# Attention over memory slots and a gated feed-forward: the sum of batch 3's nine exponentials on GpSimd, and two denominator products in place of nine

## The chip, the cores and the metric

The kernel runs on one core of a Trainium2 chip. The metric is the device time of one execution in microseconds (us). The core's engines are called PE (TensorE, matrix products), PEld (its weight loads, which run beside the products), DVE (VectorE), ACT (ScalarE), POOL (GpSimd) and SP (SyncE, which issues transfers). On-chip memory is SBUF; PE writes its results into PSUM, which has eight banks.

## The reference

There are 8 batches, 8 heads, 576 positions of 64 elements, and 32 memory slots. Per batch and head:

```python
a = exp(phi - max(phi)); a = a / (sum(a over slots) + 1e-09)
k_m = einsum('bhsm,bhsd->bhmd', a, k)        # keys of the 32 memory slots
v_m = einsum('bhsm,bhsd->bhmd', a, v)        # values of the 32 memory slots
attn = softmax(q @ k_m.T / 8)
x = attn @ v_m                               # heads side by side: 4608 x 512
out = (silu(x @ w_gate) * (x @ w_val)) @ w_out   # 512 -> 1536 -> 512
```

The kernel has its own placement of these sums: it lays heads out as 64 rows of nine positions each, and forms for every head pair and memory slot the sum of the exponentials over positions, which it calls the denominators. They scale the memory keys and values once, when these leave PSUM.

## The kernel before

**Layout.** `phi` of a batch is a tile of 128 partitions with four head pairs and nine positions (JK = 9). `phi_exp` (L170, ACT at L172) makes the exponentials `t_ephi`, 128 x (9 x 4 x 32), in bf16. A product of PE with `ones2` (two columns, one for each half of the partitions) sums them over the partitions: `kv_denominators` (L239, product at L258) does so for each of the nine positions and accumulates in PSUM, nine products of a 128 x 128 weight and two columns. `kv_sum` (L222, L230) forms the memory keys and values, 72 small products in two banks `p_kv`. `kv_reciprocal` (L260, DVE at L262) inverts the denominators and `kv_norm` (L268, DVE at L266) scales keys and values with them on their way to SBUF as `t_bkv`; `kv_T` (L278) transposes them.

**The short form.** `phi_sum(b)` (L205) lets POOL add the nine exponentials ahead of PE. Four adds at L212 (4 against 4 positions, then 2 against 2, 1 against 1, and the ninth) give one 128 x 128 sum `t_es` in fp32; a cast (L218) writes its high part and a subtract (L219) its low part, both bf16, into `t_ehl`. `kv_denominators` then makes two products, of the high and of the low part. A copy of one element, a mark (`wait_for`, L645), stands ahead of the adds, so that POOL begins with them only when the second normalised attention `t_A` of the batch in work (L452 on DVE) is there. Before the change batches 4, 6 and 7 have this form; 2, 3 and 5 make nine products; 0 and 1 have a form of their own.

**Order.** The order of each engine's instructions is written out by hand. From batch 2 on, a loop (L996) handles batch b: scores and their exponentials, sums and normalisation of the attention (L452), then the gates. `gv_gate` (L524) makes the gate and value products (L515), ACT the silu (L532), DVE the product `t_h` (L538). 24 such slots are spread with other streams by `spread` (L852): the output products of the batch before (L727), and at slots 6 to 10 `kv_items(b + 1)`, the denominators, key sums and transposes of the next batch. `kv_items` (L292) takes them in one of three ways. With a `beside` and no sum from POOL (`own`), the denominators come first, in a bank of their own `p_S`, followed by the key sums; the projections that `beside` carries (`u_item`, L472, whose results ACT and DVE copy at L492 and L496) come after. With a sum from POOL (`behind`) the key sums come first, then `beside`, then the two products into a free corner of a key bank.

**Queues.** A finished chunk of the hidden layer calls `chunk_done` (L586), which puts sums `t_S` on POOL (L603, L560), whose results the output products read, and, at chunk 1 of batch b, the loads of batch b + 3 on POOL's queue (L982: q, phi, k, v). In batch 2 POOL ends with the loads of batch 4 (L1020) ahead of the gates.

**Banks.** PSUM banks are handed out in turn from a list (L75); who takes a bank waits until its last reader is done.

Of the kernel before, what the change touches and what calls it, by code (L numbers as in the profile page):

```python
# [14 lines left out]
def kernel(  # L15
# [59 lines left out]
    def bank(shape, dtype, name):  # L75
        tag = free.pop(0)
        t = ps.tile(shape, dtype, tag=tag, name=name)
        held[id(t)] = tag, t
        return t

    def done(*tiles):

        for t in tiles:
            free.append(held.pop(id(t))[0])
# [29 lines left out]
    def load_qT(b):  # L114

        qTs[b] = att.tile([128, NS, 128], BF16, tag="qT", name="t_qT")
        nc.sync.dma_start_transpose(out=qTs[b], in_=qs[b])
# [52 lines left out]
    def phi_exp(b):  # L170
        t = att.tile([128, JK, NP, M], BF16, tag="ephi", name="t_ephi")
        nc.scalar.activation(  # L172
            out=t.rearrange("p j i m -> p i j m"),
            in_=phis.pop(b).rearrange("p i (j m) -> p i j m", m=M),
            func=AF.Exp,
        )
        ephis[b] = t
# [25 lines left out]
    esums = {}  # L203
# [18 lines left out]
    def kv_sum(b, p, parts):  # L222


        w0, w1 = parts[0], parts[-1] + 1
        n = (w1 - w0) * D
        for j in range(JK):
            for i in range(NP):
                for g in range(NG):
                    nc.tensor.matmul(  # L230
                        p[g][32 * i:32 * i + 32, 0:n],
                        lhsT=phi_of(b, g, j, i),
                        rhs=kvs[b][64 * g:64 * g + 64, w0:w1, i, j * D:(j + 1) * D],
                        start=(j == 0),
                        stop=(j == JK - 1),
                        tile_position=(64 * g, 32 * i),
                    )

    def kv_denominators(b, p):  # L239

        if b in masked:
            for g in range(NG):
                for j in range(JK):
                    nc.tensor.matmul(
                        p[:, g:g + 1],
                        lhsT=masked[b][:, j, g].rearrange("p i m -> p (i m)"),
                        rhs=ones1,
                        start=(j == 0),
                        stop=(j == JK - 1),
                    )  # L250
            return
        if b in esums:
            hl = esums.pop(b)
            terms = [hl[:, t] for t in range(2)]
        else:
            terms = [ephis[b][:, j].rearrange("p i m -> p (i m)") for j in range(JK)]
        for n, x in enumerate(terms):
            nc.tensor.matmul(p, lhsT=x, rhs=ones2, start=(n == 0), stop=(n == len(terms) - 1))  # L258

    def kv_reciprocal(b, p):  # L260
        r = att.tile([128, NG], FP32, tag="rS", name="t_rS")
        nc.vector.reciprocal(out=r, in_=p)  # L262
        rSs[b] = r
# [4 lines left out]
    def kv_norm(b, p):  # L268

        t = att.tile([128, 3, 128], BF16, tag="bkv", name="t_bkv")  # L270
        for g in range(NG):
            x = p[g][:, 0:D].rearrange("p (a d) -> p a d", a=1).to_broadcast([128, 2, D])
            scaled_copy(t[:, g].rearrange("p (a d) -> p a d", a=2), x, rSs[b][:, g:g + 1])
            scaled_copy(t[:, 2, D * g:D * g + D], p[g][:, D:2 * D], rSs[b][:, g:g + 1])
            done(p[g])
        bkvs[b] = t

    def kv_T(b):  # L278


        kTs[b] = att.tile([128, 3, 128], BF16, tag="kT", name="t_kT")
        t = bkvs.pop(b)
        if b > 3:
            nc.sync.dma_start_transpose(out=kTs[b], in_=t.rearrange("p n x -> p (n x)"))
            return
        p = bank([128, 3, 128], BF16, "p_T")
        for n in (2, 0, 1):
            nc.tensor.transpose(p[:, n], t[:, n], ident)
        nc.vector.tensor_copy(out=kTs[b], in_=p)
        done(p)  # L290

    def kv_items(b, beside=None):  # L292


        def run_sums():
            o = 2 * D
            behind = b in esums
            own = beside and not behind
            if own:
                d = bank([128, NG], FP32, "p_S")  # L300
                kv_denominators(b, d)
                kv_reciprocal(b, d)
                done(d)
            p = [bank([128, CH], FP32, f"p_kv{g}") for g in range(NG)]
            if not (own or behind):
                kv_denominators(b, p[0][:, o:o + NG])
            kv_sum(b, p, (0, 1))
            if behind:
                beside()
                kv_denominators(b, p[0][:, o:o + NG])  # L310
            if not own:
                kv_reciprocal(b, p[0][:, o:o + NG])
            kv_norm(b, p)
            if beside and not behind:
                beside()

        return [run_sums, lambda: kv_T(b)]
# [511 lines left out]
    def q_items(b, evac):  # L829
        return [lambda n=n: q_T(b, n, evac[n]) for n in range(3)]  # L830
# [30 lines left out]
    def exp_tables():  # L861
        nc.scalar.preload_act_table_set("natural_log_exp_and_others")
# [133 lines left out]
    for b in range(2, B):  # L996
        last = b + 1 == B
        exp_tables()
        if b == 2:
            load_qT(3)  # L1000
            phi_exp(2)
            (zero, ops0), (one, ops1) = products(0, ("c11",)), products(1, ("p1", "c11"))
            kv, q2 = kv_items(2), q_items(2, "aaa")
            run(zero[:6])
            sums = {n: f for n, f in zip(((1, 1), (0, 2), (1, 2)), late)}
            late.clear()
            sums[0, 2]()
            weight_sums(0)
            weight_sums(1)
            run(zero[6:12] + one[:6] + kv[:1] + q2[:2])  # L1010
            weight_sums(2, (0, 1))
            run(zero[12:16] + zero[18:22] + kv[1:] + q2[2:] + zero[16:18] + zero[22:24])
            weight_sums(2, (2, 3))
            ops0["c11"]()
            ops1["p1"]()
            wait_for(Ts[2][0:1, 3, 0, 0:1])
            for part in ((0, 1), (3,), (2,)):
                for c in (1, 2):
                    sums[1, c](part)
            loads(4)  # L1020
            backlog = one[6:12] + zero[36:] + one[12:36]
            ops = ops1
        else:
            run(take(6))
        for g in range(NG):
            scores(b, g)
        if b > 2:
            ops["p1"]()
            u_values(b)
        else:  # L1030
            run(zero[24:36] + take(6))
        run(take(6))
        z_inv_v(b, 0)
        ops["c11"]()
        run(take(6))
        if not last:
            phi_exp(b + 1)
        z_inv_v(b, 1)
        if b > 2:
            norm(b, 0)  # L1040
            norm(b, 1)
        run(take(6))
        run_late()
        if b == 4:
            wait_for(atts[4, 1][0:1, 0, 0:1])
            quad_sums(0)
        nc.scalar.preload_act_table_set("silu_and_others")
        run(take(6))
        if b == 2:
            norm(2, 0)  # L1050
        run(take(6))
        if b == 2:
            norm(2, 1)
            u_three(2)
            run(one[36:])
        g = gv_slots(b)
        quad = []
        if b == 4:
            quad = products(b, (), 0)[0]
        if last:  # L1060
            rest, rest_ops = products(b, (), 1)
            backlog += rest[:12]
        beside = 0 if last else 2 if quad else min(4, len(backlog))
        outs = [lambda: run(take(1)) for _ in range(len(backlog) - beside)]
        streams = [(g, 0, 24), (quad[:12], 0, 3), (quad[12:], 12, 18.5)]
        streams += [(outs, 4, 7 if quad else 24)]
        if b == 2:
            streams += [([lambda: u_values(2)], 2.5, 3)]
        if last:
            streams += [([u_item(b, 2)], 5, 6)]  # L1070
        if not last:
            if b > 2:
                load_qT(b + 1)
            if b > 2 and b != 4:
                phi_sum(b + 1)
            streams += [
                (kv_items(b + 1, lambda: (u_item(b, 2, "aava")(), run(take(2)))), KV, KV + 4),
                ([lambda: (u_three(b + 1), run(take(2)))], 19, 20),
            ]
        spread(*streams)  # L1080
        flush_mul()
        units, ops = products(b, ("p1", "c11"))
        backlog += units
# [34 lines left out]
```

## Time and profile before

| what | value |
|---|---|
| three timed runs | 233.22, 233.81, 233.97 us; median 233.81 |
| span of the profiled execution, first to last instruction | 231.4 us |
| its own time | not given apart; the three runs are 1.8 to 2.5 us above the span |
| mean granted TensorE clock | 0.997 |
| denominator products of batch 3 | 79.98 us from the start of the span |
| POOL idle between batch 4's loads and the first sum of batch 2 | 8.75 us, up to 83.84 us |

Times within the span count from its first instruction. A row of the timeline merges equal instructions that follow each other, and gives the start, the time from the first start to the last end, the engine, the line, the operation with what it writes and reads, and the count; in brackets stands the idle time of the engine ahead of the row, and whose end ended it. Matmuls are pipelined, so that their durations overlap: how long a product holds PE is read from the distance of the starts, not from its duration.

### The profile page before, as it was taken

What the parts mean: (1) busy time and instruction counts of PE and PEld (TensorE: products, weight loads), DVE (VectorE), ACT (ScalarE), POOL (GpSimd) and SP (SyncE); (2) the same over time, 40 slices, a digit from 0 to 9 for tenths busy, and PEclk for the clock granted to TensorE, in tenths of its full rate; (3) what the DMA queues carried; (4) which work ended last, traced back from release to release, by engine and by line L of the source; (5) the groups of instructions that cost most, each with busy time, mean ns of one, the idle gap of its engine ahead of it and who ended that gap; (6) DMA issues with size and microseconds to landing.
All of it is one profiled execution on the core that took longest, in us unless ns stands there. A gap on an engine that the chain in (4) does not pass through costs nothing.

```text
span 231.4 us, 7210 instructions
## 1 busy us (share of the span) xinstructions
PE 221.6 (96%) x2825; PEld 169.8 (73%) x2825; DVE 185.1 (80%) x423; ACT 171.7 (74%) x365; POOL 140.8 (61%) x190
## 2 busy tenths in 40 slices
PE   6987799999999999999999999999999999999993
PEld 2544476778887777878788787887788778878882
DVE  4245789999966799989997668998999899977732
ACT  2777898988447989968896658978898789677310
POOL 8422427998199049765977689464845394039291
PEclk9999999999999999999999999999999999999998
DMA  6999999999996992999299946994014502202125
GB/s 214 210 211 206 199 207 207 221 245 268 205 225 175 256 256 49 223 204 184 71 223 191 226 134 115 252 236 89 28 65 114 104 0 95 91 10 84 31 85 160
DMA packets 36674, 36.84 MB, mean 159 GB/s; under 512 B 14624, under 2 KB 31008, under 8 KB 36640
## 3 DMA queue, kind: packets, MB, share of 16 engines
q0 software_dynamic: 16272, 22.42, 52.5%
q1 hardware_dynamic: 19600, 13.18, 22.9%
q10 hardware_dynamic: 768, 0.79, 1.1%
q8 instruction: 22, 0.36, 0.6%
q14 instruction: 12, 0.10, 0.1%
HBM read 42.47 MB, written 9.44 MB: 224 GB/s over the span
## 4 chain that ended last, share of the span: by engine, by line
PE 86%; DMA 9%; POOL 2%; ACT 1%; issue 0%; DVE 0%; POOLq 0%
PE p_g L515 21%; PE p_os L727 21%; PE p_v L515 20%; PE p_oc L727 10%; DMA W<-in_moe_w_val_dram 9%; PE p_oa L727 5%; PE p_u L472 5%; PE p_kv L230 2%; PE p_g L396 1%; POOL t_kv L99 1%; POOL t_kv L103 1%; PE p_q L383 0%; POOL t_q L108 0%; ACT t_qT L337 0%; POOL W L138 0%
## 5 line engine op out<-in xcount | busy, mean ns | idle before, releaser
L538 DVE TENSOR_TENSOR t_h<-t_sg,p_v 128x288 bf16<-128x288 bf16 x192 | 81.8, 451 | 14.1 <-PE p_v L515 7.0
L515 PEld LDWEIGHTS <-t_U 128*128 128x128 bf16 x768 | 73.9, 98 | 21.2 <-issue 3.5
L532 ACT ACTIVATE t_sg<-p_g 128x288 bf16<-128x288 f32 x192 | 73.3, 424 | 17.1 <-PE p_g L515 11.4
L515 PE MATMUL p_g<-t_A,t_U 128*128 128x288 bf16 x384 | 77.0, 286 | 0.0
L515 PE MATMUL p_v<-t_A,t_U 128*128 128x288 bf16 x384 | 77.0, 286 | 0.0
L727 PEld LDWEIGHTS <-t_S 128*128 128x128 bf16 x384 | 37.5, 98 | 4.5 <-issue 0.2
L603 POOL TENSOR_TENSOR t_S<-t_h 128x512 bf16<-128x512 bf16 x17 | 19.7, 1157 | 32.7 <-DVE t_h L538 31.2
L727 PEld LDWEIGHTS <-t_h 128*128 128x128 bf16 x288 | 27.1, 98 | 8.6 <-issue 5.0
L492 ACT CAST t_U<-p_u 128x512 bf16<-128x512 f32 x51 | 27.0, 605 | 6.6 <-PE p_u L472 6.6
L727 PE MATMUL p_os<-t_T,t_S 128*128 128x256 bf16 x192 | 23.7, 273 | 0.0
L560 POOL TENSOR_TENSOR t_S<-t_S,t_h 128x512 bf16<-128x512 bf16 x17 | 19.6, 1156 | 1.3
L560 POOL TENSOR_TENSOR t_S<-t_h 128x512 bf16<-128x512 bf16 x16 | 18.4, 1152 | 0.0
L560 POOL TENSOR_TENSOR t_S<-t_h,t_S 128x512 bf16<-128x512 bf16 x16 | 18.4, 1152 | 0.0
L472 PE MATMUL p_u<-W,t_kT 64*32 64x512 bf16 (+1 forms) x416 | 15.3, 363 | 1.2 <-DMA W<-in_moe_w_gate_dram 0.6
L496 DVE CAST t_U<-p_u 128x512 bf16<-128x512 f32 x21 | 13.6, 683 | 1.9 <-PE p_u L472 1.9
L727 PE MATMUL p_os<-t_T,t_h 128*128 128x256 bf16 x96 | 14.8, 273 | 0.0
L875 PE MATMUL p_warm<-bones 128*128 128x512 bf16 x44 | 12.5, 421 | 1.7 <-DVE bones L897 1.7
L452 DVE TENSOR_TENSOR t_A<-t_E,t_lz 128x576 bf16<-128x576 bf16 x16 | 11.4, 740 | 0.7 <-ACT t_lz L428 0.7
L727 PE MATMUL p_oc<-t_T,t_S 128*128 128x256 bf16 x96 | 11.9, 273 | 0.0
L727 PE MATMUL p_oa<-WO,t_h 128*128 128x256 bf16 x96 | 11.8, 273 | 0.0
L727 PE MATMUL p_oc<-WO,t_S 128*128 128x256 bf16 x96 | 11.8, 272 | 0.1
L727 PE MATMUL p_os<-WO,t_h 128*128 128x256 bf16 x96 | 11.8, 273 | 0.0
(107 smaller groups left out, 308.3 us busy)
## 6 DMA issues: line engine op xcount, KB each, us to landing
out_dram<-t_o SPq DMA_DIRECT2D x11, 512.0 KB, 3.0
t_kv<-in_k_dram POOLq DMA_DIRECT2D x8, 576.0 KB, 10.5
t_q<-in_q_dram POOLq DMA_DIRECT2D x8, 576.0 KB, 8.4
t_kv<-in_v_dram POOLq DMA_DIRECT2D x8, 576.0 KB, 14.7
t_phi<-in_phi_dram POOLq DMA_DIRECT2D x6, 576.0 KB, 8.1
out_dram<-t_o SPq DMA_DIRECT2D x10, 256.0 KB, 4.5
WO<-in_moe_w_out_dram POOLq DMA_DIRECT2D x3, 512.0 KB, 19.2
W<-in_moe_w_gate_dram POOLq DMA_DIRECT2D x2, 512.0 KB, 16.5
```

Of the source, the lines that this page charges most:

```text
L230: nc.tensor.matmul(p[g][32 * i:32 * i + 32, 0:n], lhsT=phi_of(b, g, j, i), rhs=kvs[b][64 * g:64 * g + 64, w0:w1, i, j * D:(j + 1) * D], st ...
L452: nc.vector.tensor_tensor(out=a, in0=es.pop((b, g)), in1=lzs.pop((b, g)), op=ALU.mult)
L472: nc.tensor.matmul(p[g][32 * i:32 * i + 32, o:o + n], lhsT=kTs[b][64 * g:64 * g + 64, 2, 32 * i:32 * i + 32], rhs=w_part(w, c, i, g, halve ...
L492: nc.scalar.copy(out=t, in_=p)
L496: nc.vector.tensor_copy(out=t, in_=p)
L515: nc.tensor.matmul(p[:, 0:HALF], lhsT=Us[b, c, g][:, o // 2, which, 128 * (o % 2):128 * (o % 2 + 1)], rhs=atts[b, g][:, r], start=(g == 0) ...
L532: nc.scalar.activation(out=sg, in_=gate[:, 0:HALF], func=AF.Silu)
L538: nc.vector.tensor_tensor(out=dst, in0=sg, in1=val[:, 0:HALF], op=ALU.mult)
L560: eng.tensor_tensor(out=out, in0=x, in1=y, op=ALU.subtract)
L603: eng.tensor_tensor(out=t[:, 0], in0=A21, in1=A22, op=ALU.add)
L727: nc.tensor.matmul(mine[home][:, u], lhsT=lhs(c, m, u), rhs=rhs(c, m), start=fresh and u == 0, stop=(k == 5), skip_group_check=u == 1 or n ...
L875: nc.tensor.matmul(p[:, 0:128 * a], lhsT=bones, rhs=x.to_broadcast([128, a, 128]) if a > 1 else bones, start=True, stop=True,)
```

## The change

Two conditions change.

```diff
         def run_sums():
             o = 2 * D
-            behind = b in esums
+            behind = b in esums and b != 3
             own = beside and not behind
...
         if not last:
             if b > 2:
                 load_qT(b + 1)
-            if b > 2 and b != 4:
+            if b != 4:
                 phi_sum(b + 1)
```

The second lets `phi_sum(3)` run in batch 2, ahead of the 24 slots. The first keeps batch 3 in the `own` order although it has a sum from POOL: the denominators ahead of the key sums, in bank `p_S`. Since `esums` now holds batch 3, `kv_denominators(3)` makes two products from `t_ehl` in place of nine from `t_ephi`. All other batches keep their form.

## The prediction

> **What bounds the kernel now.** I read the busy shares of the page first, then the chain that ended last, then the timelines of TensorE (PE), GpSimd (POOL) and VectorE (DVE) around the change, and last the groups of the tiles concerned.
>
> The page of the kernel before, its busy shares and its chain of work by engine:
>
> ```profile
> PE 221.6 (96%) x2825; PEld 169.8 (73%) x2825; DVE 185.1 (80%) x423; ACT 171.7 (74%) x365; POOL 140.8 (61%) x190
> ...
> PE 86%; DMA 9%; POOL 2%; ACT 1%; issue 0%; DVE 0%; POOLq 0%
> ```
>
> PE is busy for 96% of the span and is 86% of the chain; the DMA share is the first weights, before 26.75 us. In the 40 slices the granted PE clock is 9 in all but the last. From 27 us to the last products near 227 us the group view shows idle time before PE groups of 0.6 us in all, 0.5 of it at the first projections. So a matmul that is taken away in between moves the end by its own place in the stream, and a wait put there moves it by its length. POOL at 61% is off the chain.
>
> PE at the place of the change, timeline of the kernel before (start us, duration us, engine, line, operation, count; one row merges equal instructions that follow each other):
>
> ```profile
> 79.73 0.41 PE L515 MATMUL p_v<-t_A,t_U 128*128 128x288 bf16 x2
> 79.98 0.37 PE L258 MATMUL p_S<-ones,t_ephi 128*128 128x2 bf16 x9
> 80.28 0.80 PE L230 MATMUL p_kv<-t_kv,t_ephi 64*32 64x128 bf16 x72
> 80.86 0.66 PE L472 MATMUL p_u<-W,t_kT 64*32 64x512 bf16 x16
> ```
>
> The nine denominator products stand in a bank of their own already, ahead of the 72 key sums, with no idle time before them. The order of PE's instructions in the two built kernels differs by 14 rows, seven weight loads and seven matmuls, all here; the order of banks is the same.
>
> **PE's part.** The nine last 0.37 us together and one alone 163 ns (the group of L258), so eight steps take 0.207 us: 26 ns from one to the next; the single starts, 79.978, 80.007, 80.032 up to 80.182, give 25. From the ninth start to the first key sum (80.275) are 93 ns, a change of tile shape that stays. So 9 to 2 products saves 7 x 25 ns = **0.175 us**, if nothing makes PE wait. The second product would then start at 80.007 and the key sums at 80.10.
>
> A row sets the far end. A weight load of L258 lasts 95 to 98 ns. If the loads could not overlap, seven would be worth 7 x 96 ns = 0.67 us. The starts 25 ns apart speak against it, so I take 0.175 and keep 0.67 for the low end of the range.
>
> [...]
>
> **Does the earlier end reach the end of the kernel?** After the key sums the next waits are for banks. Ends of DVE and ACT (ScalarE) work against PE starts, singly in the trace: the projections (L472) at 80.86 to 81.09 take banks that were free by 80.01, 80.13, 80.38 and 80.44, at least 0.65 us before each start; the bank of the second key sum was freed 0.45 us before it. A shift of 0.175 fits into these. The tightest comes later: the weight load at 82.17 comes 0.05 us after the last normalisation (L266) ended at 82.11. That chain shifts too, because its first instruction waits for the key sums themselves:
>
> ```profile
> 80.66 0.16 DVE L262 RECIPROCAL t_rS<-p_S 128x2 f32<-128x2 f32 x1
> 81.12 0.99 DVE L266 TENSOR_SCALAR t_bkv<-p_kv,t_rS 128x128 bf16<-128x128 f32 x4 [0.30 <-PE p_kv L230]
> ```
>
> DVE stands idle for 0.30 us here until the key sums end, and the reciprocal is over at 80.82. With key sums 0.175 earlier it starts at 80.95, still after the reciprocal. ACT's next copies (81.39, idle 0.95 us before) wait for PE as well. So the whole wave moves, and behind it every stage is paced by PE.
>
> **POOL's part.** The order view puts seven instructions on POOL: a mark (L645), four adds (L212), a cast (L218) and a subtract (L219), between the batch-4 loads and the first sum t_S of batch 2 (L603). The first two rows below are these neighbours; the others are the same seven instructions where batch 4 has them now:
>
> ```profile
> 74.34 0.76 POOL L103 DMA_DIRECT2D t_kv<-in_v_dram  x1
> 83.84 1.15 POOL L603 TENSOR_TENSOR t_S<-t_h 128x512 bf16<-128x512 bf16 x1 [8.75 <-DVE t_h L538]
> ...
> 99.54 0.18 POOL L645 COPY t_mark<-t_A 1x1 bf16<-1x1 bf16 x1 [2.49 <-DVE t_A L452]
> 99.68 1.15 POOL L212 TENSOR_TENSOR t_es<-t_ephi 128x512 f32<-128x512 bf16 x1
> 100.91 1.26 POOL L212 TENSOR_TENSOR t_es<-t_es 128x256 f32<-128x256 f32 x2
> 102.25 0.43 POOL L212 TENSOR_TENSOR t_es<-t_es,t_ephi 128x128 f32<-128x128 f32 x1
> 102.74 0.29 POOL L218 CAST t_ehl<-t_es 128x128 bf16<-128x128 f32 x1
> 103.11 0.43 POOL L219 TENSOR_TENSOR t_ehl<-t_es,t_ehl 128x128 bf16<-128x128 f32 x1
> ```
>
> From the mark's start to the end of the cast are 103.03 - 99.54 = 3.49 us, to the end of the subtract 103.54 - 99.54 = **4.00 us** (3.99 and 4.00 in batches 6 and 7). POOL has an idle gap of 8.75 us to hold it. The mark waits for the second normalisation of batch 2:
>
> ```profile
> 74.90 0.75 DVE L452 TENSOR_TENSOR t_A<-t_E,t_lz 128x576 bf16<-128x576 bf16 x1
> ```
>
> It ends at 75.65. In batch 4 that instruction ended at 99.41 and the mark began at 99.54, 0.13 later; 0.13 in batches 6 and 7 too. So the mark starts at 75.78, the high part (cast) is there at 79.27 and the low part (subtract) at **79.78**. The exponentials themselves (L172) were done at 72.04.
>
> PE loads the high part at 79.86 (the first L258 load of before) and the low part at 79.98 (the second). The margins are 0.59 and **0.20 us**. A releaser's end to PE's start takes between 0.05 us (the product at 75.04 after DVE's 74.99) and 0.13 (DVE to POOL above), so 0.07 to 0.15 us remain. It is narrow, but I cost the wait at nothing. If that cover is gone, PE stands for what is missing, with all 72 key sums behind the waiting load in its queue.
>
> How sure is 4.00? POOL's 66 sums of t_S last 1142 to 1172 ns under whatever DVE and ACT do beside them, so 2% or 0.08 us is the spread to expect. That leaves the margin at about zero in the worst case, hence a lost gain of up to 0.1 us. What this stage has and batch 4 has not is two DVE casts (L496, 75.57 to 76.85) beside the first adds. If each blocked POOL for its whole 0.68 us, the low part would come at 81.14. The nearest rows say no: POOL sums beside the three casts at 88.64 to 90.52 last 1.15 to 1.16. I take nothing, and keep 1.36 us as the upper end.
>
> [...]
>
> Queued behind the mark on POOL is the L603 sum at 83.84. POOL would be free at 79.78, 4.06 us ahead of it; without that cover its sums and the batch-5 loads at 91.47 would be late by what is missing. No DMA is added or moved; SP's order is the same. DVE beside such adds is not slowed: six products of L538 take 2.91 us from 100.64, 455 ns each, as they do at 79.56 with POOL idle. The buffer of these exponentials is written again by batch 5 at 120.2, long after POOL's last read.
>
> **Sum.** 0 on POOL, DVE, ACT and SP, -0.175 on PE: the span goes from 231.4 to 231.3 us. Three times are given, 233.22 to 233.97, none named as that of the profiled execution; what lies around the span is 1.8 to 2.5 us, 2.4 by the median, and doesn't change. So **233.6 us** against 233.81.
>
> **Rivals.**
> 1. *The products' loads are worth their full length.* 0.67 us less, 233.1. For it: the 96 ns of a load. Against: the 25 ns between starts, and PEld is at 73%, not the limit.
> 2. *The low part arrives a little late or PE's queue runs dry at the wait.* With 0.1 to 0.4 us of standing the gain is used up: 233.7 to 234.0. For it: a margin of 0.07 to 0.15 us, and PE now has to take up 144 loads and matmuls of key sums straight behind a wait. Against: three chains of 3.99 to 4.00.
> 3. *Slower: the two casts block POOL.* Place: the first adds, 75.8 to 78. Low part at 81.14, PE starts its load 0.05 later, 81.14 + 0.05 - 79.98 = 1.21 us of standing, less 0.175: +1.03, 234.8. It decides once the chain is longer than 4.00 + 0.15 + 0.175, some 4.3 us, and passes 0.3% (0.70 us) at some 5.0. Against: the sums beside casts above.
> 4. *The change doesn't do what it says*, nine products kept: excluded by the order of instructions.
>
> **Chances.** Forecast 0.78, rival 1 0.05, rival 2 0.10, rival 3 0.07. A change of 0.3% is about what a measurement of this kernel can tell from no change: 233.11 and 234.51 are its bounds. Forecast and rival 2 lie within; rival 1 is on the lower bound and counts as faster, rival 3 as slower: 0.05, 0.88, 0.07. The range: the runs of before lie 0.59 below to 0.16 above their median, which makes 233.0 to 233.8 of the forecast; rival 2 and the same scatter extend it to 234.2, rival 1 lies inside, rival 3 outside.
>
> **What would show it.** Right: a mark near 75.8 and L219 ending near 79.8 on POOL; two L258 products from 79.98 with no idle time before the weight loads; key sums at 80.10; the projections at 88.09 0.17 earlier, and so to the end. Wrong: a PEld wait on POOL at L258, an L212 of over 1.2 us, L538 above 460 ns beside it, or a later PE wait that takes the 0.17 back.

## The result, and the profile after

The changed kernel takes 232.91 us (median of 17 runs, 232.83 to 233.39); the kernel before, run beside it, 233.41 (17 runs, 233.14 to 233.97). The ratio is **0.9982** (95% interval 0.9976 to 0.9988): 0.42 us less, between 0.28 and 0.56 (the medians lie 0.50 apart). The forecast was 0.175 us less. The size is wrong by a factor of 2.4, and the 233.6 us also stood on a median of three runs, 233.81, that 17 runs put at 233.41.

The page after, the busy shares and the chain by engine:

```profile
PE 222.2 (96%) x2818; PEld 169.8 (73%) x2818; DVE 184.9 (80%) x423; ACT 171.7 (74%) x365; POOL 144.3 (62%) x197
...
PE 86%; DMA 9%; POOL 2%; ACT 1%; issue 0%; DVE 0%; POOLq 0%
```

PE has seven products less and POOL seven instructions more, 3.5 us of work; the shares are as before. PE at the place of the change, timeline after:

```profile
79.67 0.41 PE L515 MATMUL p_v<-t_A,t_U 128*128 128x288 bf16 x2
79.91 0.19 PE L258 MATMUL p_S<-ones,t_ehl 128*128 128x2 bf16 x2
80.03 0.80 PE L230 MATMUL p_kv<-t_kv,t_ephi 64*32 64x128 bf16 x72
80.62 0.66 PE L472 MATMUL p_u<-W,t_kT 64*32 64x512 bf16 x16
```

Two products, no idle time ahead of them, and the key sums 0.12 us after the first (0.30 before). This execution reaches the stretch 0.064 us earlier than that of before, an amount that it has from the very start, ahead of 26 us. From the first gates to the key sums it needs 0.177 us less, and from there to the last product 147.05 us as before. DVE behind it:

```profile
74.84 0.75 DVE L452 TENSOR_TENSOR t_A<-t_E,t_lz 128x576 bf16<-128x576 bf16 x1
80.59 0.16 DVE L262 RECIPROCAL t_rS<-p_S 128x2 f32<-128x2 f32 x1
80.88 0.99 DVE L266 TENSOR_SCALAR t_bkv<-p_kv,t_rS 128x128 bf16<-128x128 f32 x4
```

The idle time ahead of the normalisation, 0.30 us, is gone: it starts 0.24 us earlier, with the key sums. The normalised attention `t_A`, for which POOL's mark waits, ends at 75.59. POOL after:

```profile
74.27 0.76 POOL L103 DMA_DIRECT2D t_kv<-in_v_dram  x1
75.65 0.18 POOL L645 COPY t_mark<-t_A 1x1 bf16<-1x1 bf16 x1 [0.62 <-DVE t_A L452]
75.79 1.15 POOL L212 TENSOR_TENSOR t_es<-t_ephi 128x512 f32<-128x512 bf16 x1
77.02 1.25 POOL L212 TENSOR_TENSOR t_es<-t_es 128x256 f32<-128x256 f32 x2
78.35 0.43 POOL L212 TENSOR_TENSOR t_es<-t_es,t_ephi 128x128 f32<-128x128 f32 x1
78.85 0.29 POOL L218 CAST t_ehl<-t_es 128x128 bf16<-128x128 f32 x1
79.21 0.43 POOL L219 TENSOR_TENSOR t_ehl<-t_es,t_ehl 128x128 bf16<-128x128 f32 x1
83.59 1.15 POOL L603 TENSOR_TENSOR t_S<-t_h 128x512 bf16<-128x512 bf16 x1 [3.95 <-DVE t_h L538]
```

The chain takes 79.64 - 75.65 = 3.99 us beside the two casts. It ends at 79.64, 0.27 us ahead of the load that needs it (79.91), and POOL still waits 3.95 us for its next sum.

So the two profiles show the forecast 0.18 us at its place and nothing more between 27 and 227 us. The other 0.24 us of the ratio are not in these two executions.

### The profile page after: what moved, and what is told of

It is laid out like the page before. It is cut to its first block, busy times and chain, and to the rows that moved or that the text cites. A ratio compares the mean times of both kernels' runs of the same rounds, so it can differ in the third digit from the quotient of the medians.

```text
span 231.1 us, 7204 instructions
## 1 busy us (share of the span) xinstructions
PE 222.2 (96%) x2818; PEld 169.8 (73%) x2818; DVE 184.9 (80%) x423; ACT 171.7 (74%) x365; POOL 144.3 (62%) x197
## 4 chain that ended last, share of the span: by engine, by line
PE 86%; DMA 9%; POOL 2%; ACT 1%; issue 0%; DVE 0%; POOLq 0%
PE p_g L515 21%; PE p_os L727 21%; PE p_v L515 20%; PE p_oc L727 10%; DMA W<-in_moe_w_val_dram 9%; PE p_oa L727 5%; PE p_u L472 5%; PE p_kv L230 2%; PE p_g L396 1%; POOL t_kv L99 1%; POOL t_kv L103 1%; PE p_q L383 0%; POOL t_q L108 0%; ACT t_qT L337 0%; POOL W L138 0%
## 5 line engine op out<-in xcount | busy, mean ns | idle before, releaser
L515 PEld LDWEIGHTS <-t_U 128*128 128x128 bf16 x768 | 73.9, 98 | 21.2 <-issue 3.5
L515 PE MATMUL p_g<-t_A,t_U 128*128 128x288 bf16 x384 | 77.0, 286 | 0.0
L515 PE MATMUL p_v<-t_A,t_U 128*128 128x288 bf16 x384 | 77.0, 286 | 0.0
L875 PE MATMUL p_warm<-bones 128*128 128x512 bf16 x44 | 13.5, 447 | 1.7 <-DVE bones L897 1.7
```

Of the source, the lines that this page charges most:

```text
L515: nc.tensor.matmul(p[:, 0:HALF], lhsT=Us[b, c, g][:, o // 2, which, 128 * (o % 2):128 * (o % 2 + 1)], rhs=atts[b, g][:, r], start=(g == 0) ...
L875: nc.tensor.matmul(p[:, 0:128 * a], lhsT=bones, rhs=x.to_broadcast([128, a, 128]) if a > 1 else bones, start=True, stop=True,)
```

## The experiments

**Theories.** Theory 1: PE's 0.18 us is all, and the rest is scatter. Theory 2: something else of the change gives 0.2 to 0.3 us, by POOL's work (2b) or by the missing PE instructions (2a). Theory F, formed after the first two sets: PE's instructions come to it by transfers, and in part of the runs of the kernel before one of these comes late; the change moves the place where it is needed. Each set of runs has its own runs of the kernel before on the same chip, and each ratio is to these; not every set has runs of the changed kernel.

### Controls and halves

Before again: no edit.

> The kernel before, unchanged, against itself: how far two sets of runs of one kernel lie apart on this chip. All theories: ratio 1.000, with the interval across 1. If it lies beside 1 by 0.05% or more, a difference of the size of 0.1 us cannot be put down to a change at all.

Measured: 1.0004 (0.9991 to 1.0018). The changed kernel again:

> The changed kernel once more. In its first profile the PE stream is 0.18 us shorter at the denominators of batch 3, as predicted, while the time fell by 0.42 us (ratio 0.9982, 0.9976 to 0.9988). Theory 1 (the change is worth the 0.18 us of PE alone, and the rest is scatter of the parts ahead of 26 us and behind 227 us, which differs from one set of runs to the next): ratio near 0.9992, anywhere from 0.998 to 1.000. Theory 2 (something of the change outside the PE stretch gives 0.2 to 0.3 us more, each time): 0.9982 again, and the profile again shows it in the same part.

Measured: 0.9982 (0.9973 to 0.9991), 233.12 us. So the size repeats. PE's part without POOL's (seven of batch 3's nine positions are left out of the sums):

```diff
-            terms = [... for j in range(JK)]
+            terms = [... for j in range(2 if b == 3 else JK)]
```

> The kernel before, with the denominators of batch 3 summed from two positions of nine: seven of nine are left out, and POOL adds nothing. Theory 1: as the changed kernel, 0.18 us less on PE, ratio near 0.9992. Theory 2a (the extra comes from seven fewer PE instruction pairs): as the changed kernel, 0.9982. Theory 2b (the extra comes from POOL's work): 0.9992 while the changed kernel stays at 0.9982.

Measured: 0.9981 (0.9971 to 0.9991). POOL's part without PE's:

```diff
+            if b != 4:
                 phi_sum(b + 1)
+            if b == 2:
+                esums.pop(3)
```

> The kernel before, with POOL's sum of the exponentials of batch 3 made in batch 2 as in the change, but not used: batch 3 keeps its nine products. Theory 1 and 2a: ratio 1.000, PE's stream unchanged to 0.02 us. Theory 2b: 0.9988 to 0.9990, that is 0.25 us less without any product saved. Rival 3 of the prediction (POOL and DVE in each other's way): slower, L538 or L496 longer by more than 10 ns beside the adds.

Measured: 1.0003 (0.9988 to 1.0017). POOL's work alone gives nothing that these runs can tell, and costs nothing; the whole 0.42 to 0.44 us come with the seven missing PE products. Theory 2b falls, 2a stands.

The profile of this run with POOL's sum alone fell on a run of 234.40 us, and shows where such runs lose their time. PE there, and in the kernel before at the same place:

```profile
134.92 0.41 PE L515 MATMUL p_v<-t_A,t_U 128*128 128x288 bf16 x2
136.29 0.71 PE L727 MATMUL p_oc<-t_T,t_Q 128*128 128x256 bf16 x5 [0.97 <-issue]
```

```profile
134.85 0.41 PE L515 MATMUL p_v<-t_A,t_U 128*128 128x288 bf16 x2
135.09 0.71 PE L727 MATMUL p_oc<-t_T,t_Q 128*128 128x256 bf16 x5
```

From one row's start to the next are 1.37 us in place of 0.24: PE stands for 1.13 us, and the bracket names no engine and no transfer of data, but issue, the profile's word for a wait whose cause it doesn't show. Theory F holds that PE lacks its own instructions. The page lists a queue for instructions:

```profile
q8 instruction: 22, 0.36, 0.6%
```

These are 22 transfers of 16,384 bytes; PE's list has 5668 rows in the trace, so one for about every 258; two places at which PE stands, both shown below, lie 768 numbers and three transfers apart, which makes 256. That they carry PE's instructions is inferred from these numbers and from what follows. Their times are in the trace. The one that starts at 132.3 in the kernel before lands at 133.51, and the instruction at 135.09, number 3522 in PE's list, runs without delay; in the run of 234.40 us it starts at 133.73, lands at 134.97, and number 3522 runs at 136.29. In the changed kernel the list is 14 shorter ahead of this point, so that number 3522 is seven products later in the work, at 135.64:

```profile
135.40 0.41 PE L515 MATMUL p_g<-t_A,t_U 128*128 128x288 bf16 x2
135.64 0.41 PE L515 MATMUL p_v<-t_A,t_U 128*128 128x288 bf16 x2
```

Landing of that transfer and first use of number 3522, us, in nine of the profiles:

| profile | number 3522 as in | landing | use | between | PE stands there |
|---|---|---|---|---|---|
| before | before | 133.51 | 135.09 | 1.59 | 0 |
| before again | before | 133.66 | 135.16 | 1.51 | 0 |
| POOL's sum alone | before | 134.97 | 136.29 | 1.32 | 1.13 |
| two products, seven more early | before | 133.96 | 135.28 | 1.32 | 0.28 |
| nine, seven more early | work 14 places later | 133.95 | 135.25 | 1.30 | 0.78 |
| the same again | work 14 places later | 131.79 | 134.42 | 2.63 | 0 |
| after | after | 133.41 | 135.64 | 2.23 | 0 |
| after again | after | 133.67 | 135.76 | 2.09 | 0 |
| after, third | after | 134.34 | 135.89 | 1.55 | 0 |

In the three profiles in which PE stands here, it stands at number 3522, which is another product where the list ahead of it is longer, and goes on 1.30 to 1.32 us after the landing; no profile shows a shorter distance at this number. The kernel before has 0.2 to 0.3 us to spare over that, the changed one 0.2 to 0.9. In all other profiles of this case, those of the sections below included, the distance is 1.73 us or more. In all, three of the seven profiles with the list of before or a longer one show PE standing there, and none of the eleven with a shorter list. The run of 234.40 us less its 1.13 us is 233.27, as the profiled run of before again (233.28), in which PE doesn't stand.

The place matters because PE uses up its list unevenly. From number 3266, 256 places ahead, PE takes 6.04 us to number 3522 in the kernel before and 6.72 in the changed one: with seven products fewer ahead, the first of these places comes 0.11 us later in the work, since small products stand there (72 key sums in 0.73 us), and the second 0.79 us, since large ones do (two of L515 in 0.24 us).

### Moving the list of instructions

If F holds, it is the place in the list that counts, not the product saved. The warming products are products of PE on a constant, which `warm` issues while inputs are on their way; `warm(104)` makes 26 of them, 512 columns wide, and a second argument asks for that many of 128 columns. Seven warming products less at the start, nine denominator products kept:

```diff
-    warm(104)
+    warm(76)
```

> The kernel before with its nine products, and seven of the 26 warming products at the start of PE (ahead of 9 us, while the inputs are on their way) taken away, so that everything behind them stands 14 places earlier in PE's list of instructions, as it does in the changed kernel. Theory F (fetch): PE's instructions come in 22 transfers of 16 KB, and in the kernel before the instruction at 135.1 us is the first of such a transfer, which landed 1.5 to 1.6 us ahead of it, and in one profile 1.3 us ahead with PE standing for 1.13 us; with 14 places less that first instruction comes 0.5 to 0.6 us later in the work, and the standing goes. It expects 0.2 to 0.3 us less than before (ratio 0.9987 to 0.9992) although no product of batch 3 is saved, no run above 233.7, and 2.0 us or more between landing and use. Theory 1 (PE's 0.18 us and scatter): ratio 1.000. If the shorter warming lowers the granted clock, it is slower by a us or more and the run tells nothing.

Measured: 1.0014 (0.9999 to 1.0028), an expectation missed. In its profile the first gates start at 27.80 us, 0.6 late, behind weights that came late (PE waits 1.25 us for them, 0.52 in the kernel before); from the key sums of batch 3 on it takes 147.06 us, with 2.56 from landing to use. The start spoilt it, and the time says nothing of F. Seven more in the changed kernel:

```diff
-    warm(104)
+    warm(111, 7)
```

> The changed kernel with seven narrow products more among the warming ones at the start, so that the work behind batch 3 stands at the same places in PE's list of instructions as in the kernel before. Theory F: the 0.18 us of the seven products stay, the rest goes: ratio to before 0.9992 (233.3 where before has 233.5), scattered runs above 233.8 return, 1.5 to 1.6 us between landing and use at 135. Theory 2a without the fetch (fewer products give 0.43 us in some other way): 0.9982 as the changed kernel.

Measured: 0.9992 (0.9983 to 1.0002), 233.25 us, with one run at 233.92. Its profile shows PE standing again:

```profile
134.76 0.41 PE L515 MATMUL p_v<-t_A,t_U 128*128 128x288 bf16 x2
135.28 0.71 PE L727 MATMUL p_oc<-t_T,t_Q 128*128 128x256 bf16 x5
```

0.52 between the rows in place of 0.24. F gave 0.9992, the products alone in another way 0.9982, which the interval leaves out by little; it does not leave out 1.000, and this set has no runs of the changed kernel. The same edit in the kernel before:

> The kernel before with seven narrow products more at the start: 14 places later in PE's list. Theory F: the first instruction of that transfer is now needed some 0.7 us earlier, near 134.4, 0.8 to 0.9 us after the landing where 1.3 are needed, so PE stands in every run, 0.4 us at the least, and more where the transfer is late: ratio 1.002 to 1.004, and the profile shows idle PE ended by issue near 134.4. Theory 1 and any theory without the fetch: ratio 1.000.

Measured: 0.9995 (0.9986 to 1.0003), against F. Its profile was of its longest run, 234.23 us, and there number 3522, seven products earlier in the work and due at 134.4, does wait, for 0.78 us:

```profile
134.25 0.38 PE L727 MATMUL p_os<-t_T,t_Q 128*128 128x256 bf16 x2
135.25 0.38 PE L727 MATMUL p_os<-t_T,t_Q 128*128 128x256 bf16 x2 [0.62 <-issue]
```

The other eleven, 233.07 to 233.66, leave no room for such a wait: the lowest run of the kernel before in this set is 233.09. (The 0.86 us of the next expectation is the whole stretch behind the key sums; 0.08 of it arises near 111.5 us, in the repeat as well.) Once more, for a profile of one of those:

> The kernel with seven narrow products more at the start once more. Its first 12 runs contradicted theory F: median 0.1 us below before in place of 0.4 to 0.9 above, although its one profile (a run of 234.23) shows PE standing for 0.86 us at 134.4, 1.30 us after the landing. Theory F, kept: a profile of a run near 233.3 shows the transfer landing at 133.0 or earlier, so that 1.3 us remain. Theory F, fallen: a run near 233.3 with the landing at 133.5 as in the kernel before and no standing.

Measured: 0.9995 (0.9984 to 1.0006). The profiled run, 233.36 us, had the landing at 131.79, as F needs. In this run the transfer started at 130.86, some 1.5 us ahead of its start in the kernel before; I had held that start for fixed, and the size that F gave for these two sets is refuted with it: the place alone doesn't say how long PE stands. The attempt to shorten the list at the other end of the start:

```diff
     z_inv(1, 0)
-    warm(8)
     z_inv(1, 1)
     norm(1, 0)
-    warm(16)
+    warm(4)
     v_direct(1, "vvvv")
-    warm(8)
```

> The kernel before with nine products and seven of the 512-wide warming products between 21 and 25 us left out (the first attempt took them from the very start and delayed the first projections by 0.5 us). Everything from 26 us on stands 14 places earlier in PE's list. Theory F: 2.0 us or more from landing to use at 135, no standing there, ratio 0.9987 to 0.9992 if the first gates stay near 27.2 us and the stretch from there to the key sums of batch 3 stays at 53.07 us; if these move, the rest behind batch 3 is to be compared alone: 147.05 us in the profile. Theory 1: 1.000.

Measured: 1.0044 (1.0017 to 1.0071), with 4 of 12 runs at 233.12 to 233.37 and 8 at 234.25 to 236.13. Stretches of its profile; the columns are stretch, length, then busy time of PE, PEld, DVE, ACT and POOL, the granted clock, DMA share and GB/s:

```profile
26.00:27.40 1.40, 1.09 (x32) 0.39 (x31) 1.00 (x2) 0.96 (x3) 0.99 (x2) 0.50 1.45 196
27.40:28.20 0.80, 0.80 (x12) 0.52 (x5) 0.80 (x3) 0.80 (x3) 0.48 (x1) 0.50 1.41 200
```

The kernel before at its first gates:

```profile
27.20:28.20 1.00, 1.00 (x17) 0.80 (x10) 1.00 (x3) 1.00 (x3) 0.74 (x1) 1.00 1.40 203
```

The granted clock is 0.50 where the kernel before has 1.00. Over whole runs, the eight long ones have a mean clock of 0.983 to 0.993, the four short ones 0.997 to 1.000. So the median says nothing of F. The four runs with the clock kept lie 0.15 to 0.4 us below the 233.52 of the kernel before, about where F puts them, but four runs picked by their clock prove little.

### Less traffic ahead of the transfer

The store of 512 KB issued near 124 us is left out, with nine products and with two (256 positions of batch 3 are then missing from the output):

```diff
     def store_block(t_o, b, n, cols):
+        if (b, n) == (3, 0):
+            return
```

> The kernel before with its nine products, without the store of 512 KB that SP issues near 124 us (256 positions of batch 3 are not written). [...] Theory F: with less traffic ahead of it the transfer lands earlier, 0.3 us or more ahead of the 133.5 of before, PE's standing at 135.1 goes, and the time falls by 0.2 to 0.3 us without any product saved: ratio 0.9987 to 0.9992, no run above 233.7. Theory 1 (PE's 0.18 us and scatter ahead of 26 us): ratio 1.000 and the same spread of runs as before. If the store has no part in it: 1.000, and the transfer lands at 133.5.

Measured: 0.9993 (0.9982 to 1.0004); landing at 132.50, 2.64 us ahead of the use, and one run above 233.7 (233.92).

> The changed kernel without the same store. Theory F: as the changed kernel, 0.9982, since PE doesn't stand there any more; its distance to the nine products without the store shrinks to the 0.18 us of the products (0.08%), from 0.43. Theory 2a without the fetch: the distance to the nine products without the store stays 0.43 us.

Measured: 0.9978 (0.9967 to 0.9989). Nine products have a median 0.2 us lower without the store (233.31 against 233.52), but the interval of their ratio includes 1; two products stand at 233.12, the median of the changed kernel in the second set (this set has no runs of it). The distance between the two is 0.19 us by the medians, 0.35 by the ratios, so it doesn't decide between the 0.18 of the products and 0.43. The transfer landed a microsecond earlier in the one profile of nine products; but with the store in place it has landed as early as 131.79. That the store or batch 7's loads hold the transfer up was my guess, and the kernel before doesn't show it: there their last packets end at 130.98 and 130.66, 1.3 us ahead of the transfer's start at 132.32.

### The same PE work, another place in the list

Seven products less in batch 3, seven more in batch 6:

```diff
-        else:
+        if b == 6 or b not in (3, 4, 7):
             terms = [ephis[b][:, j]... for j in range(JK)]
```

> The changed kernel a third time, as the base for the three others of this set: ratio 0.9982, no run above 233.5, 2.0 us or more from the landing to the first use near 135.6.

Measured: 0.9972 (0.9961 to 0.9984), 233.03 us, the kernel before here at 233.63; 1.55 us from landing to use in place of the 2.0 expected, since the transfer started at 133.16.

> The changed kernel with the denominators of batch 6 made of nine products in place of two, at the place that batch 6 has for them (POOL's sum for it is made and not used): seven products are taken away in batch 3 and seven are added in batch 6 near 156 us, so PE's work is that of the kernel before, while at 135 us the list of instructions stands as in the changed kernel. Theory F: the 0.18 us are lost again and the rest stays: ratio to before 0.9988 to 0.9991, no run above 233.7, 0.18 us above the changed kernel. Theory 1 (PE's work alone, the rest is scatter): 1.000. A gain of 0.43 us in proportion to the products: 1.000 as well.

Measured: **0.9980** (0.9971 to 0.9989), 233.26 us, no run above 233.43. PE does the products of the kernel before, the nine of batch 6 among them,

```profile
157.16 0.37 PE L258 MATMUL p_kv<-ones,t_ephi 128*128 128x2 bf16 x9
```

and its profile needs 147.23 us from the key sums to the end of the products, 0.18 more than 147.05. It is still 0.47 us faster than the kernel before (0.26 to 0.68), and 0.23 slower than the changed one. PE's work alone, which expected 1.000, falls: most of the gain stays when the work of the seven products is put back behind 135 us. Seven products fewer in batch 2 as well, by two of nine positions in its sums:

```diff
-                for j in range(JK)
+                for j in range(2 if b == 2 else JK)
```

> The changed kernel with the denominators of batch 2 summed from two positions of nine (seven are left out), near 58 us: 14 places and 0.175 us less once more. Theory F: PE doesn't stand at 135 any more, so the second step is worth its 0.175 us alone: ratio to before 0.9974 to 0.9975, to the changed kernel 0.9992. A gain in proportion to the products: another 0.43 us, 0.9963.

Measured: 0.9965 (0.9951 to 0.9978; 5 runs), 0.13 us below the changed kernel of the same set. Seven more products saved are worth 0.13 us by the medians and 0.16 by the ratios, a rough figure with five runs, and not another 0.43.

### The bank of their own

```diff
-            behind = b in esums and b != 3
+            behind = b in esums
```

> The changed kernel with the other order for batch 3: key sums first, then the projections, then the two products in a key bank, as batches 4, 6 and 7 have it. PE's count is the same, so theory F and theory 1 expect no more than 0.1 us between the two orders, if no wait comes of it; what could make it slower is that the normalisation of keys and values starts behind the projections, some 0.6 us later than now, and the gates that take its banks wait: 0.3 us or more of idle PE between 81.5 and 83 would show it (ratio to before 0.9995 or more).

Measured: 1.0022 (1.0011 to 1.0032), 234.13 us, 1.1 above the changed kernel. DVE's reciprocal and PE's weight loads in that order:

```profile
82.02 0.16 DVE L262 RECIPROCAL t_rS<-p_kv 128x2 f32<-128x2 f32 x1
82.31 0.10 PEld L515 LDWEIGHTS <-t_U 128*128 128x128 bf16 x1 [0.27 <-issue]
83.26 0.17 PEld L288 LDWEIGHTS <-t_bkv 128*128 128x128 bf16 x3 [0.86 <-DVE t_bkv L266]
```

The reciprocal comes behind the projections and a cast (82.02 in place of 80.59), the normalisation with it, and the transposes of PE wait 0.6 us for it. The second half of the change's first line is worth 1.1 us, which the prediction did not price.

This profile has one more stand of PE, a short one, at number 2754, three times 256 places ahead of number 3522; its transfer, the third ahead of the one above, landed at 105.12, 0.83 us before this load:

```profile
105.95 0.36 PEld L515 LDWEIGHTS <-t_U 128*128 128x128 bf16 x4 [0.18 <-issue]
```

So the 1.3 us are not a fixed distance.

### How near the wait is

```diff
         add(t, e[:, 0:4], e[:, 4:8])
+        if b == 3:
+            add(t, e[:, 0:4], e[:, 4:8])
```

> The changed kernel with the first add of POOL's sum of batch 3 made twice (the same result): the low part is ready 1.15 + 0.08 us later, near 80.87 in place of 79.64. How near is the wait that the prediction costed at nothing? If the margin is the 0.27 us from the subtract's end to the load that needs it less 0.05 to 0.13 of releasing, PE stands for 1.23 - 0.27 + 0.05 to 0.13 = 1.0 to 1.1 us at the second L258 load, and the time rises by the same over the changed kernel: 234.0 to 234.1 where that has 233.0, ratio to before 1.002 to 1.003. If the wait were covered by more than that, or PE made up for it behind, less than 0.5 us.

Measured: 1.0025 (1.0015 to 1.0034), 234.05 us. POOL's subtract and PE's weight loads (L260, L220 and L221 here are L258, L218 and L219):

```profile
80.47 0.43 POOL L221 TENSOR_TENSOR t_ehl<-t_es,t_ehl 128x128 bf16<-128x128 f32 x1
80.45 0.10 PEld L260 LDWEIGHTS <-t_ehl 128*128 128x128 bf16 x1 [0.65 <-POOL t_ehl L220]
80.95 0.10 PEld L260 LDWEIGHTS <-t_ehl 128*128 128x128 bf16 x1 [0.41 <-POOL t_ehl L221]
```

The subtract ended at 80.90, the second load follows 0.05 later, and from the key sums of batch 2 to those of batch 3 are 22.71 us, against 21.71 in the changed kernel. That is the expected 1.0 to 1.1: of the 1.23 us 0.23 were covered, and the rest is paid in full.

## Why the prediction was wrong in size

- **PE's part was right.** 0.175 us forecast, 0.177 in the profiles. The rival of 0.67 us is refuted by the profile, though the time came near its 233.1.
- **The passage to the later stages was right as far as it went.** The normalisation moved with the key sums, and 147.05 us behind them did not change.
- **POOL's part was right.** 4.00 us forecast, 3.99 measured beside the two casts, so rival 3 didn't come about; POOL's sum alone gives 1.0003, and PE took up the key sums behind the wait without a gap (rival 2). The wait was costed at nothing and cost nothing; its margin, 0.07 to 0.15 us by the prediction, was 0.23, since the mark followed DVE by 0.06 and not 0.13 us.
- **The step that failed** is "every stage is paced by PE", with its premise that a matmul taken away moves the end by its own place in the stream. That holds in the profiled execution, in which PE happened not to stand. In others PE stands at number 3522 of its list, for 1.13 us in the longest case of three, and the profile names nothing that releases it. The prediction had the 14 rows in hand and took them for the time of seven products alone; their other effect, that number 3522 is used 0.6 us later (0.79 of work less 0.18), it put at nothing. The missing term is 0.24 us in two of the sets (0.42 less 0.18) and 0.47 in the third (0.65 less 0.18).
- **The base was too high.** Of the 0.7 us between the forecast 233.6 and the measured 232.91, 0.4 are the median of three runs, 233.81 in place of 233.41, and 0.3 the size of the change. The scatter of these three, 233.22 to 233.97, was taken for scatter around the span. It was a sign: of the 149 runs of the kernel before that stand beside the others, 56 are above 233.6; of the 79 in seven sets of kernels whose list stands at 135 as in the changed one or shorter and whose start is untouched (the changed one three times, two products alone, nine in batch 6, batch 2 as well, two without the store), none is.

What stays open. That PE stands at number 3522 is shown by three profiles, one with PE's list of the kernel before (POOL's sum alone), none of the kernel before itself. How often and for how long was not counted, since one profile is had of each kernel, so the 0.24 to 0.47 us are a difference and not a sum of waits. The three sets that hold both kernels (81 and 41 runs together) agree with waits in part of the runs: the kernel before lies 0.69 us above the changed one at the point that a tenth of the runs exceed, 0.48 at the median and 0.29 at the point that a tenth stay below. The last is more than 0.18, so a tenth of a us may have another source. Theory F as first stated, in which the place in the list alone decides, did not hold: seven products more ahead of nine should have cost 0.4 us or more and cost nothing, and the attempts with seven fewer were spoilt by their start. What sets the start of the transfer, between 130.9 and 133.7, is not settled: in one profile each without the store it started at 131.4 and 131.6, but in the list with seven more it started at 130.86 with the store in place.

## What to carry to other kernels

Where PE is busy for 96% of the span and runs of one kernel differ by more than the profile explains, look for idle PE ended by "issue" in a profile of a long run, and at the instruction queue's transfers beside it: here a stretch with many small products used up 256 places of PE's list in 6.04 us in the kernel before, and in three profiles of other kernels PE stood behind this stretch until 1.30 to 1.32 us after 16 KB had landed; that it lacked instructions is my inference. In this kernel the number of instructions ahead of the place counted as well as their time, and the edit that shortens the list was worth more than its products (0.42 to 0.65 us against 0.18). Spend several runs of the kernel before on its scatter before giving a forecast of 0.1%.

## What the runs showed of the hardware that I had not expected

- PE stood three times at number 3522 of its list, for 0.28, 0.78 and 1.13 us, until 1.30 to 1.32 us after 16 KB had landed, whatever product the number was; a short stand, at number 2754, with 0.18 us of idle time, ended 0.83 us after its own 16 KB. That PE lacked instructions is inferred from these distances.
- Seven 512-wide warming products fewer between 21 and 25 us left the clock at 0.50 at the first gates in the profile, and 8 of 12 runs took 0.7 us or more longer than the median of the kernel before.
- The first transposes of batch 2's queries wait for their load in some profiles: by 0.24 us in the changed kernel's third, by 0.30 in that of nine products without the store, not in those of the kernel before and of the first run of the changed one:

```profile
59.30 0.67 PEld L383 LDWEIGHTS <-t_q 128*128 128x128 bf16 x12 [0.24 <-DMA t_q<-in_q_dram]
```
